# A planner with a stricter PSUM rule and another transfer model, and 48 sums made by GpSimd instead of VectorE

## The chip, the cores and the metric

The kernel runs on one core of a Trainium2 chip. A core has five engines that run side by side, each in the order of its own queue: TensorE (matrix products, "PE" in the profile, with its weight loads as "PEld"), VectorE ("DVE"), ScalarE ("ACT"), GpSimd ("POOL") and SyncE ("SP"), which here only issues transfers. Operands lie in SBUF, 128 partitions wide; TensorE writes its sums into PSUM. What is measured is the device time of one execution, in microseconds (us). Comparisons use the median of several executions.

## The reference

The kernel computes a gated mix of two branches over the same `x` (2048 rows, 1024 columns), all in fp32:

```python
g = sigmoid((x * gate_w).sum(-1, keepdims=True))
a = x @ hid_re.T;  b = x @ hid_im.T              # [2048, 1024] each
A = seq_re @ a - seq_im @ b                      # real part of the 2-D Fourier mixing
h = relu(x @ w1 + b1) ** 2                       # [2048, 3584]
B = h @ w2 + b2
out = g * A + (1 - g) * B
```

The four matrices of the Fourier part come in as inputs. The result is needed in fp32 accuracy.

## The kernel before, in words

**Products.** TensorE multiplies in a reduced fp32 format, so every fp32 operand is split in two: `hi`, a copy rounded to that format (ScalarE, `Operand.sum_parts`, line 297), and `lo = operand - hi` (VectorE, `Operand.rest_parts`, line 306). A product of two operands is three matrix products, hi·lo, hi·hi and lo·hi. To do fewer of them the kernel uses Strassen's scheme in Winograd's form: seven products of half-sized blocks instead of eight, with four sums on the left side (`SUMS_L`: S1 to S4), four on the right (`SUMS_R`: T1 to T4, lines 36 to 39), and adds of the results. Many of the seven products are themselves made by the same scheme once more ("twice", second level); the others are made directly.

**Stages.** The work is four matrix products one after the other: x (x times the hidden Fourier matrices, function `x_stage`), c (the sequence Fourier matrices times that, `c_stage`), h in two parts (x times `w1`, `h_stage`), and o (`w2` times h, `o_stage`). Stages x and h run through `wide`, c and o through `tall`. In each the seven products are done in the order 1, 2, 5, 6, 3, 7, 4. In `tall` the constants `TWICE_C` and `TWICE_O` (line 21) say which are done twice and over how many of their k-steps: in c products 1 (one double step), 2, 3 and 4 (four double steps each, which is all of them); in o product 1 (two) and 2, 3 and 4 (three double steps, six of the seven k-steps). What is left of the k-steps (`rest` in `tall.twice`, lines 523 to 532) is done plainly: before the second level when the product starts from nothing or is named in `FIRST_C` / `FIRST_O` (line 22), otherwise after it. With `rest` done first, an extra set of PSUM groups takes it up and writes it to SBUF, and the second level is put on top. With `rest` done last, its matrix products go into the same PSUM groups as the second level's products 2, 3 and 4, and into a fourth group for the block (1, 1) (lines 614 to 636). The last product of the last stage (o, product 4) ends in a group that hands over each of its two rows by itself (`by_row`, lines 608 to 610); which group that is depends on whether `rest` comes last.

**One second level step.** For each double step q of a twice-product in `tall`, the left operand's blocks lie in two tiles, and `l2[q]` (line 543) makes the sums S1 to S4 of their halves, each 128x512 elements (two tiles of 256 columns). S1 and S3 take two loaded blocks, S2 needs S1, S4 needs S2. The sum itself is issued in `Part.make_parts` (line 257), by VectorE. In stages c and o that is 13 + 11 = 24 double steps. The right sums are 128x1024 each.

**PSUM.** PSUM is used as four pools, each a tile of 128x2x512 fp32, so of two rows of 128x512. A group's result is taken up by VectorE or ScalarE. In o's `final` (line 881) the two rows of a tile are finished by two `scalar_tensor_tensor` instructions (bias and gate), one per row, then one add of the whole tile, and the tile goes out through a store on GpSimd's queue. `last` (line 866) does the same for a single row, with the store on SyncE's or ScalarE's queue.

**The order of the work.** Nothing is issued while the program is described: every instruction is recorded as an `Op` (line 99) with its time by a table of costs (lines 27 to 30), and with the earlier ops that it must follow (`Queue`, lines 139 to 146). `plan` (line 973) then gives every op a due time, counted back from the matmuls, which are to run without a pause, and simulates the engines: when an engine is free it takes the ready op that is due first. Matmuls keep their recorded order. SBUF is 55 slots of 128x1024 fp32; a tile gets its slot in the order of due time less a lead (`LEAD`), and a load can't be issued before its tile has a slot. `emit` writes the instructions out in the order of the planned starts, one fixed queue per engine. The engines then run for real in these orders, with waits wherever a tile is shared, so what the plan gets wrong shows up as a wait. All instructions carry the line of the call in `emit`, L1125, so the profile tells them apart by tile names: `raw` is a loaded block, `sum` a sum, `hi`, `lo` the halves of an operand (`both` for the 256-wide ones), `ps` a PSUM tile, `u`, `ab`, `y`, `h`, `o` results, `copy` a sum kept in DRAM.

Of the kernel before, what the change touches and what calls it, by code (L numbers as in the profile page):

```python
# [15 lines left out]
P = 128  # L16
# [2 lines left out]
SLOTS = 55  # L19
WIDE, TALL_C, TALL_O = ((1, 2, 5, 6, 3, 7, 4),) * 3  # L20
TWICE_X, TWICE_C, TWICE_O = (1, 2, 5, 3, 4), {1: 1, 2: 4, 3: 4, 4: 4}, {1: 2, 2: 3, 3: 3, 4: 3}
FIRST_C, FIRST_O = (2,), (2, 4)
WARM = 44
FAR_TALL, FAR_WIDE = ("T2",), ()
TWICE_H = (1, 2, 5, 3, 4), (1, 2, 5, 3, 4)

MM, MM_END, FIRST_MM = 0.2267, 0.18, 6.2
VEC, VEC_END, ACT, ACT_END = (0.086, 1.0417e-3), 0.39, (0.11, 0.89e-3), 0.36
ISSUE, RING, RATE, SEM, LANES = {"sync": 0.36, "scalar": 0.36, "gpsimd": 0.56}, (1.1, 1.1), 400e3, 0.06, 8
LEAD = {"raw": 5.0, "hi": 5.0, "sum": 5.0, "out": 0.0}  # L30

ADD, SUB = ALU.add, ALU.subtract

# [2 lines left out]
SUMS_L = {"S1": ((1, 0), (1, 1), ADD), "S2": ("S1", (0, 0), SUB), "S3": ((0, 0), (1, 0), SUB),  # L36
          "S4": ((0, 1), "S2", SUB)}
# [7 lines left out]
def gated_mix_kernel(ctx: ExitStack, tc: tile.TileContext, x4, xn, w4, ct, w1a, w1b, w2, b1, b2, gw, out):  # L45
# [11 lines left out]
    class Sight:  # L57


        def __init__(self, base, chain, box):  # L60
            self.base, self.chain, self.box = base, chain, box
# [12 lines left out]
        def __getattr__(self, name):  # L74
            def later(*args, **kwargs):
                return Sight(self.base, self.chain + (lambda t: getattr(t, name)(*args, **kwargs),), self.box)
            return later
# [21 lines left out]
    class Op:  # L99


        def __init__(self, engine, name, args, kwargs):
            self.engine, self.name, self.args, self.kwargs = engine, name, args, kwargs
            sights = [a for a in (*args, *kwargs.values()) if isinstance(a, Sight)]
            outs = [a for a in (args[0], kwargs.get("accum_out")) if isinstance(a, Sight)]
            self.ins, self.outs = [a for a in sights if not any(a is o for o in outs)], outs
            n = max([a.size() for a in sights] + [0])
            self.load, self.end = 0.0, 0.0
            if name == "dma_start":
                self.time, self.load = ISSUE[engine], n * P * 4 / RATE  # L110
            elif engine == "tensor":
                self.time, self.end = (MM, MM_END) if n >= 512 else (0.13, 0.1)
            elif engine == "scalar":
                self.time, self.end = ACT[0] + ACT[1] * n + (1.3 if args[2] == AF.Sigmoid else 0.0), ACT_END
            elif name == "tensor_scalar":
                self.time, self.end = VEC[0] + VEC[1] * n / 2, VEC_END
            else:
                self.time, self.end = VEC[0] + VEC[1] * n, VEC_END
            self.after, self.then, self.new, self.latest, self.landed = set(), [], [], None, False
# [3 lines left out]
    class Queue:  # L123
# [5 lines left out]
        def __getattr__(self, name):  # L129
            def record(*args, **kwargs):  # L130
                op = Op(self.engine, name, args, kwargs)
                op.latest = urgent[0]
                for sight, write in [(a, False) for a in op.ins] + [(a, True) for a in op.outs]:
                    block = sight.base
                    if not block.seen and block.home in ("slot", "bank"):
                        op.new.append(block)
                    if not block.seen and block.before is not None:
                        op.after.update(o for o, *_ in block.before.seen)
                    for other, box, wrote in block.seen:
                        if (write or wrote or block.home == "bank") and (not box or not sight.box or (  # L140
                                box[0] < sight.box[1] and sight.box[0] < box[1] and (
                                    block.home == "bank" or box[2] < sight.box[3] and sight.box[2] < box[3]))):
                            op.after.add(other)
                    block.seen.append((op, sight.box, write))
                op.after.discard(op)
                ops.append(op)
                return op
            return record
# [4 lines left out]
    nc = Machine()  # L153
# [19 lines left out]
    def take(name, dtype=F32):  # L173
        return Block(name, dtype, "slot")
# [50 lines left out]
    class Part(Near):  # L225


        def __init__(self, a, b=None, op=None, width=512):
            super().__init__("part")
            self.blocks, self.op, self.width, self.copy = ([a] if b is None else [a, b]), op, width, None  # L230
            self.cuts = [(slice(0, 2), slice(0, width))]
            for e in self.blocks:
                if isinstance(e, (Near, View)):
                    e.uses += 1
# [14 lines left out]
        def make_parts(self):  # L249
            for b in self.blocks:  # L250
                assert not isinstance(b, (Near, View)) or b.done
            src = [b.slot if isinstance(b, (Near, View)) else t for b, t in zip(self.blocks, self.slots)]
            mine = [t for t in self.slots if t is not None]
            self.slot, self.done = mine[0] if mine else take("sum"), True
            for k, c in self.cuts:
                if self.op:
                    nc.vector.tensor_tensor(self.slot[:, k, c], src[0][:, k, c], src[1][:, k, c], op=self.op)
                yield
            for b in self.blocks:
                if isinstance(b, (Near, View)):  # L260
                    b.used()
            if self.copy:
                stores.append((self.copy, self, 0, 2))
# [53 lines left out]
    class Half:  # L317
# [6 lines left out]
        hi = property(lambda self: self.base.hi[:, :, self.at:self.at + 256])  # L324
# [70 lines left out]
    class Sums:  # L395


        def __init__(self, get, sums, keep=False, far=()):

            self.get, self.sums, self.keep, self.far, self.made = get, sums, keep, far, {}  # L400

        def of(self, key, width=512, near=False):
            if key in self.made:
                return self.made[key]
            if key not in self.sums:
                if not self.keep:
                    return self.get(*key)
                b = self.get(*key)
                e = b if isinstance(b, (Near, View)) else Part(b, width=width)
            else:  # L410
                a, b, op = self.sums[key]
                e = Part(*(self.of(p, width).far() if p in self.far and not near else self.of(p, width) for p in (a, b)), op, width)
            self.made[key] = e
            return e

# [55 lines left out]
    def tall(left, right, ksteps, order, second, first, target, final, last=None):  # L471
# [46 lines left out]
        def twice(p, old, new, ends, drop, sign):  # L518
# [3 lines left out]
            k = second[p]  # L522
# [16 lines left out]
            def near(b):  # L539
                return b if isinstance(b, Near) else Part(b)  # L540

            base = {(j, q): near(left[2 * q + j].of(l)) for j in range(2) for q in range(k)}
            l2 = {q: Sums(lambda m, j, q=q: View(base[j, q], 256 * m), SUMS_L, True) for q in range(k)}
            r2 = {q: Sums(lambda j, c, q=q: right[2 * q + j, c].of(r), SUMS_R, True) for q in range(k)}

            def one(_, ps):
# [88 lines left out]
            for e in own:  # L635
                step(*e)

        return seven(order, second, lambda: {k: Near("u") for k in keys}, c11, c12, c21, c22, put, add, direct, twice, 2)

    def wide(left, right, rows, order, second, target, final, sign=1, onto_old=False):  # L640
# [264 lines left out]
    at, rows = c_stage()  # L905
# [5 lines left out]
    at, rows, fetched, ends = o_stage()  # L911
# [31 lines left out]
    ideal, t = [], FIRST_MM  # L943
# [29 lines left out]
def plan(ops, count, start):  # L973

    t = start
# [20 lines left out]
    def lead(op, block):  # L996
        kind = "raw" if op.load else "out" if any(a.base.home == "bank" for a in op.ins) else "hi"
        return op.due - LEAD[kind]

# [10 lines left out]
    moving, at, version = {}, 0.0, 0  # L1010
    lanes = [], []

    def push(t, *what):
        heappush(events, (t, len(events) + 1e-9 * len(order), id(what), what))
# [5 lines left out]
    def loosen(op):  # L1020
        op.wait -= 1
        if not op.wait:
            able(op)

    def hand_out():
        nonlocal head
        while head < len(queue) and free:
# [2 lines left out]
            head += 1  # L1030
            loosen(op)

    def flow(t):
        nonlocal at, version
        for e in moving:
            moving[e][1] -= (t - at) / len(moving)
        at = t
        version += 1
        for e in [e for e in moving if moving[e][1] <= 1e-9]:
            op = moving.pop(e)[0]  # L1040
            push(t + RING[1], "done", op)
        for e, r in rings.items():
            if e not in moving and r:
                op = r.popleft()
                moving[e] = [op, op.load]
        if moving:
            push(t + max(0.0, min(m[1] for m in moving.values())) * len(moving), "flow", version)

    def finish(op):
        op.landed = True  # L1050
# [116 lines left out]
```

## Time and profile before

| | us |
|---|---|
| median of 3 executions (1870.84 to 1874.90) | 1872.18 |
| the profiled execution | 1871.76 |
| its span, first to last instruction | 1869.6 |
| TensorE busy | 1852.4 |
| VectorE busy | 1761.1 |
| ScalarE busy | 1086.2 |
| GpSimd busy | 87.6 |

The profile is of one execution. Its rows give the time that each engine worked, and the idle time ahead of an instruction with what ended it ("<-DVE o" means that VectorE's last write or read of a tile `o` released it). A matmul record lasts about 390 ns while the next starts after about 227 ns, since matmuls are pipelined; so a pause of TensorE is read from the distance between starts. In the timeline each line has the start, the length, the engine, the operation, the tiles and, in brackets, the idle time just before. In a table by stretches each engine has its busy time and, in brackets, its instructions.

The boundaries of the products in stage o, by counting matmuls (one product of 300, three of 336, and so on) back from the last: product 1 about 1356 to 1427, product 2 to 1495, product 5 to 1571, product 6 to 1648, product 3 to 1719, product 7 to 1795, product 4 to the end. In stage c, which ends about 863, product 3 takes about 623 to 700.

### The profile page before, as it was taken

To read this page: it belongs to the slowest core of one execution; us is meant where nothing else is said; L and a number is where in the kernel's file an instruction comes from. 1 tells how busy PE (TensorE), PEld (TensorE's weight loads), DVE (VectorE), ACT (ScalarE), POOL (GpSimd) and SP (SyncE) were. 2 spreads that over 40 slices of the span, in tenths; PEclk is the share of its full clock that TensorE was granted. 3 is DMA by queue.
4 is the path that set the end of the run, shared out by engine and by line. 5 is a ranking of instruction groups with operands and counts; after the bars stand their busy time and mean duration, and the time that the engine had idled before them with its cause. 6 is when DMAs were issued, how large, how long until landed. Compare 5 with 4: busy or idle time off the path is not lost. (4 is left out here: it accounts for less than half of the span.)

```text
span 1869.6 us, 22164 instructions
## 1 busy us (share of the span) xinstructions
PE 1852.4 (99%) x8162; PEld 1529.5 (82%) x8162; DVE 1761.1 (94%) x1728; ACT 1086.2 (58%) x1231; POOL 87.6 (5%) x162
## 2 busy tenths in 40 slices
PE   9999999999999999999999999999999999999998
PEld 7888888888888888888888888788887888887887
DVE  8997998999889899999997999999999998989988
ACT  6474554563343554466584798767977435364462
POOL 0000100000000000000000001000010000000000
PEclk9999999999999999999999999999999999999999
DMA  4641979449798379444551845737664798649952
GB/s 180 259 169 67 352 264 385 159 152 409 266 324 324 136 268 411 158 166 168 219 198 56 333 170 184 270 122 284 240 240 172 288 386 317 269 146 380 363 180 90
DMA packets 128860, 445.04 MB, mean 238 GB/s; under 512 B 14176, under 2 KB 23664, under 8 KB 128752
## 3 DMA queue, kind: packets, MB, share of 16 engines
q1 hardware_dynamic: 106848, 365.10, 53.1%
q0 software_dynamic: 21616, 78.14, 10.6%
q8 instruction: 64, 1.05, 0.2%
q10 hardware_dynamic: 288, 0.39, 0.1%
q14 instruction: 44, 0.36, 0.1%
HBM read 364.92 MB, written 78.65 MB: 237 GB/s over the span
## 5 line engine op out<-in xcount | busy, mean ns | idle before, releaser
L1125 PE MATMUL ps<-hi 128*128 128x512 f32 x2034 | 793.5, 391 | 6.5 <-DVE h L1125 2.6
L1125 PE MATMUL ps<-hi,lo 128*128 128x512 f32 x2034 | 792.9, 390 | 1.7 <-DVE o L1125 1.7
L1125 PE MATMUL ps<-lo,hi 128*128 128x512 f32 x2034 | 792.4, 390 | 0.0
L1125 ACT ACTIVATE hi<-raw 128x1024 fp32r<-128x1024 f32 (+2 forms) x384 | 394.2, 1037 | 341.7 <-DVE raw L1125 212.1
L1125 DVE TENSOR_TENSOR lo<-raw,hi 128x1024 fp32r<-128x1024 f32 (+2 forms) x384 | 454.1, 1200 | 13.4 <-ACT hi L1125 10.7
L1125 PEld LDWEIGHTS ps<-hi 128*128 128x128 f32 x2034 | 382.5, 188 | 88.9 <-ACT hi L1125 4.0
L1125 PEld LDWEIGHTS ps<-hi,lo 128*128 128x128 f32 x2034 | 382.5, 188 | 82.7 <-DVE o L1125 2.6
L1125 PEld LDWEIGHTS ps<-lo,hi 128*128 128x128 f32 x2034 | 382.5, 188 | 79.5 <-DVE lo L1125 0.2
L1125 PE MATMUL ps<-hi,both 128*128 128x512 f32 x1344 | 416.1, 390 | 2.5 <-ACT ps L1125 2.5
L1125 DVE TENSOR_TENSOR raw<-raw 128x1024 f32<-128x1024 f32 (+1 forms) x276 | 327.6, 1209 | 28.1 <-DMA raw<-in_ct 11.7
L1125 ACT ACTIVATE hi<-sum 128x1024 fp32r<-128x1024 f32 x216 | 219.6, 1034 | 157.5 <-DVE sum L1125 111.0
L1125 PEld LDWEIGHTS ps<-hi,both 128*128 128x128 f32 x1344 | 252.3, 188 | 56.1 <-ACT ps L1125 3.8
L1125 DVE TENSOR_TENSOR lo<-sum,hi 128x1024 fp32r<-128x1024 f32 (+1 forms) x216 | 255.1, 1198 | 13.5 <-PE ps L1125 7.4
L1125 PE MATMUL ps<-lo,both 128*128 128x512 f32 x672 | 261.7, 389 | 0.0
L1125 DVE TENSOR_TENSOR sum<-raw 128x1024 f32<-128x1024 f32 (+2 forms) x156 | 160.9, 1041 | 8.3 <-PE ps L1125 4.4
L1125 ACT ACTIVATE u<-ps 128x1024 f32<-128x1024 f32 (+1 forms) x116 | 112.2, 972 | 71.4 <-PE ps L1125 53.6
L1125 PEld LDWEIGHTS ps<-lo,both 128*128 128x128 f32 x672 | 126.2, 188 | 26.0
L1125 DVE TENSOR_TENSOR sum<-raw,sum 128x1024 f32<-128x1024 f32 (+2 forms) x117 | 128.7, 1103 | 7.2 <-PE ps L1125 6.1
L1125 DVE TENSOR_TENSOR h<-h,ps 128x1024 f32<-128x1024 f32 (+1 forms) x92 | 98.7, 1085 | 8.7 <-ACT u L1125 6.2
L1125 ACT ACTIVATE ps<-u 128x1024 f32<-128x1024 f32 (+1 forms) x84 | 82.1, 980 | 29.2 <-DVE o L1125 7.4
L1125 ACT ACTIVATE both<-sum 128x512 fp32r<-128x512 f32 x96 | 59.3, 626 | 66.0 <-DVE sum L1125 54.0
L1125 ACT ACTIVATE h<-h,b1c 128x512 f32<-128x512 f32 x112 | 75.7, 710 | 10.0 <-DVE h L1125 9.9
(47 smaller groups left out, 731.5 us busy)
## 6 DMA issues: line engine op xcount, KB each, us to landing
raw<-in_ct SPq DMA_DIRECT2D x153, 512.0 KB, 6.7
raw<-h SPq DMA_DIRECT2D x134, 512.0 KB, 7.3
raw<-in_x SPq DMA_DIRECT2D x107, 512.0 KB, 5.5
raw<-in_w SPq DMA_DIRECT2D x98, 512.0 KB, 7.1
raw<-ab SPq DMA_DIRECT2D x72, 512.0 KB, 7.1
h<-h POOLq DMA_DIRECT2D x48, 512.0 KB, 5.3
raw<-in_w1a SPq DMA_DIRECT2D x36, 512.0 KB, 6.2
ab<-ab POOLq DMA_DIRECT2D x32, 512.0 KB, 7.0
```

The source lines that it names most:

```text
L1125: made = getattr(real[op.engine], op.name)(*(actual(a) for a in op.args), **{k: actual(v) for k, v in op.kwargs.items()})
```

## The change

Five edits in one:

1. `FIRST_O` loses product 4: its left-over k-step is now done after the second level, as product 3's is. So the kernel's last group becomes the block (1, 1) with one k-step (12 matmuls), after three groups of 12 matmuls that end blocks (0, 0), (1, 0) and (0, 1).
2. In the recording of dependencies, any two accesses to the same PSUM tile are now ordered in the plan, reads against reads and the two rows of a tile against each other. Before, only accesses to overlapping rows were.
3. ScalarE is counted as 0.11 + 0.84e-3 n (before 0.89e-3) with 0.41 at the end (0.36). A transfer is counted with 1.6 us ahead and 2.0 behind (1.1 and 1.1), at 405e3 bytes per us alone and 370e3 shared (400e3).
4. Tiles that are loaded get their slot 9 us ahead of the due time, not 5.
5. S1 and S3 of the second level in `tall` are issued on GpSimd: 24 double steps, two sums each, 48 adds of 128x512. The plan counts each as 0.3 + 2.2e-3 n.

```diff
-FIRST_C, FIRST_O = (2,), (2, 4)
+FIRST_C, FIRST_O = (2,), (2,)
...
-VEC, VEC_END, ACT, ACT_END = (0.086, 1.0417e-3), 0.39, (0.11, 0.89e-3), 0.36
-ISSUE, RING, RATE, SEM, LANES = {"sync": 0.36, "scalar": 0.36, "gpsimd": 0.56}, (1.1, 1.1), 400e3, 0.06, 8
-LEAD = {"raw": 5.0, "hi": 5.0, "sum": 5.0, "out": 0.0}
+VEC, VEC_END, ACT, ACT_END = (0.086, 1.0417e-3), 0.39, (0.11, 0.84e-3), 0.41
+ISSUE, RING, RATE, SEM, LANES = {"sync": 0.36, "scalar": 0.36, "gpsimd": 0.56}, (1.6, 2.0), (405e3, 370e3), 0.06, 8
+POOL = 0.3, 2.2e-3
+LEAD = {"raw": 9.0, "hi": 5.0, "sum": 5.0, "out": 0.0}
...
-                self.time, self.load = ISSUE[engine], n * P * 4 / RATE
+                self.time, self.load = ISSUE[engine], n * P * 4 / RATE[0]
...
+            elif engine == "gpsimd":
+                self.time, self.end = POOL[0] + POOL[1] * n, VEC_END
...
-                        if (write or wrote or block.home == "bank") and (not box or not sight.box or (
-                                box[0] < sight.box[1] and sight.box[0] < box[1] and (
-                                    block.home == "bank" or box[2] < sight.box[3] and sight.box[2] < box[3]))):
+                        if block.home == "bank" or (write or wrote) and (not box or not sight.box or (
+                                box[0] < sight.box[1] and sight.box[0] < box[1] and box[2] < sight.box[3]
+                                and sight.box[2] < box[3])):
                             op.after.add(other)
...
-        def __init__(self, a, b=None, op=None, width=512):
+        def __init__(self, a, b=None, op=None, width=512, adder=nc.vector):
             super().__init__("part")
+            self.adder = adder
...
-                    nc.vector.tensor_tensor(self.slot[:, k, c], src[0][:, k, c], src[1][:, k, c], op=self.op)
+                    self.adder.tensor_tensor(self.slot[:, k, c], src[0][:, k, c], src[1][:, k, c], op=self.op)
...
-        def __init__(self, get, sums, keep=False, far=()):
+        def __init__(self, get, sums, keep=False, far=(), other=()):
+            self.other = other
...
-                e = Part(*(self.of(p, width).far() if p in self.far and not near else self.of(p, width) for p in (a, b)), op, width)
+                e = Part(*(self.of(p, width).far() if p in self.far and not near else self.of(p, width) for p in (a, b)), op, width,
+                         nc.gpsimd if key in self.other else nc.vector)
...
-            l2 = {q: Sums(lambda m, j, q=q: View(base[j, q], 256 * m), SUMS_L, True) for q in range(k)}
+            l2 = {q: Sums(lambda m, j, q=q: View(base[j, q], 256 * m), SUMS_L, True, other=("S1", "S3")) for q in range(k)}
...
+    def share():
+        return 1.0 if len(moving) == 1 else len(moving) * RATE[0] / RATE[1]
+
     def flow(t):
         nonlocal at, version
         for e in moving:
-            moving[e][1] -= (t - at) / len(moving)
+            moving[e][1] -= (t - at) / share()
...
-            push(t + max(0.0, min(m[1] for m in moving.values())) * len(moving), "flow", version)
+            push(t + max(0.0, min(m[1] for m in moving.values())) * share(), "flow", version)
```

## The prediction

> **What bounds the kernel now.** I read the page first, then the table by stretches, the waits of TensorE, and the timeline around each of its pauses.
>
> ```profile
> span 1869.6 us, 22164 instructions
> PE 1852.4 (99%) x8162; PEld 1529.5 (82%) x8162; DVE 1761.1 (94%) x1728; ACT 1086.2 (58%) x1231; POOL 87.6 (5%) x162
> ```
> ```profile
> core 0: us, PE busy (x) PEld busy (x) DVE busy (x) ACT busy (x) POOL busy (x), PEclk, DMA share, GB/s
> 288.80:863.40 574.60, 574.60 (x2536) 475.93 (x2536) 537.82 (x543) 282.82 (x317) 17.07 (x32) 1.00 0.68 255
> 1427.00:1495.20 68.20, 68.20 (x302) 56.52 (x301) 67.77 (x76) 41.14 (x50) 0.71 (x1) 1.00 0.66 241
> 1647.60:1719.00 71.40, 68.86 (x301) 56.04 (x300) 68.27 (x72) 38.51 (x44) 0.09 (x1) 1.00 0.67 248
> 1141.00:1353.00 212.00, 208.22 (x914) 170.96 (x913) 203.20 (x211) 165.21 (x210) 14.01 (x26) 1.00 0.62 222
> 630.00:716.00 86.00, 86.00 (x381) 71.25 (x380) 85.69 (x90) 48.16 (x56) 1.60 (x3) 1.00 0.68 260
> ```
>
> TensorE works 1852.4 of 1869.6 us, always at the full granted clock, and the number of its matmuls does not change. So no edit can win more than its pauses. In stage c (288.8 to 863.4) there is none at all. Stage o's product 2 (1427 to 1495) shows the unhindered pace: 300 matmuls in 68.20 us, 0.227 us each. Product 3 has 300 too and takes 71.40 us: 3.2 us of pauses. VectorE is the second bound. It works 67.77 of 68.20 us in o's product 2, 85.69 of 86.00 around c's product 3: where both levels of sums are made it has no time of its own left, and the kernel lives on the lead it built up before.
>
> How small that lead becomes is read by pairing an operand's `lo` with the matmul that takes it, in the queues' fixed orders. These are the tightest pairs, first in c's product 3, then in o's product 2:
>
> ```profile
> 671.94 1.29 DVE L1125 TENSOR_TENSOR both<-raw,both 128x512 fp32r<-128x512 f32 x2
> 676.00 0.61 PE L1125 MATMUL ps<-hi,both 128*128 128x512 f32 x2
> ...
> 1489.80 0.69 DVE L1125 TENSOR_TENSOR both<-sum,both 128x512 fp32r<-128x512 f32 x1
> 1492.95 0.62 PE L1125 MATMUL ps<-hi,both 128*128 128x512 f32 x2
> ```
>
> The first of the two at 671.94 ends at 672.6, its matmul starts at 676.0: 3.4 us. In o it is 2.5 us. VectorE may fall back that far, less some 0.3 us of handover, before TensorE stops.
>
> **The change, part by part.**
>
> *The PSUM rule.* Product 3 of o has these pauses:
>
> ```profile
> 1706.93 0.39 PE L1125 MATMUL ps<-lo,hi 128*128 128x512 f32 x1
> 1707.35 0.75 DVE L1125 SCALAR_TENSOR_TENSOR o<-ps,b2c,g 128x512 f32<-128x512 f32 x1 [0.23 <-PE ps L1125]
> ...
> 1708.16 0.50 PE L1125 MATMUL ps<-hi,lo 128*128 128x512 f32 x1 [0.85 <-DVE o L1125]
> ...
> 1711.57 0.51 PE L1125 MATMUL ps<-hi 128*128 128x512 f32 x1 [0.84 <-DVE o L1125]
> ...
> 1715.25 0.51 PE L1125 MATMUL ps<-hi,lo 128*128 128x512 f32 x1 [0.84 <-DVE o L1125]
> ```
>
> Six matmuls fill row 0 of a tile, VectorE starts to read row 0, and TensorE then waits with row 1 of the same tile until that read has ended. The old plan let VectorE in between because the rows differ; the built program makes TensorE wait for the whole tile. Under the new rule the first `scalar_tensor_tensor` follows row 1's matmuls, so all three pauses go: minus 3.2 us by the table. What is late next is the block's end, by row 1's six matmuls (1.36 us); product 7 behind it needs a tile only after the next group's 2.7 us, which covers that.
>
> *Product 4 of o, left-over step last.* It loses a set of groups: four copies into PSUM, four out, against one copy more at the end, all on ScalarE, which works 36.5 us in the last 74 and covers either. Its second-level products then follow in the order 2, 4, 3 (block (1, 0) before (0, 1)) where now 4 comes last. That hits one pause:
>
> ```profile
> 1841.08 1.03 ACT L1125 ACTIVATE ps<-o 128x1024 f32<-128x1024 f32 x1 [2.28 <-DVE o L1125]
> 1841.20 0.39 PE L1125 MATMUL ps<-hi,both 128*128 128x512 f32 x1
> 1842.16 0.50 PE L1125 MATMUL ps<-hi,both 128*128 128x512 f32 x1 [0.57 <-ACT ps L1125]
> ```
>
> Here block (0, 1)'s copy is needed 2.7 us after product 5 has ended; later it is needed after 5.4. The pause is 1842.16 − 1841.20 − 0.23 = 0.7 us, and goes. Cost: the end.
>
> ```profile
> 1857.62 1.40 DVE L1125 SCALAR_TENSOR_TENSOR o<-ps,b2c,g 128x512 f32<-128x512 f32 x2
> ...
> 1859.06 1.22 DVE L1125 TENSOR_TENSOR o<-o,raw 128x1024 f32<-128x1024 f32 x1
> ...
> 1863.83 0.39 PE L1125 MATMUL ps<-hi,both 128*128 128x512 f32 x1
> 1864.29 0.74 DVE L1125 SCALAR_TENSOR_TENSOR o<-ps,b2c,g 128x512 f32<-128x512 f32 x1
> 1865.07 0.69 DVE L1125 TENSOR_TENSOR o<-o,raw 128x512 f32<-128x512 f32 x1
> 1865.79 0.35 ACTq L1125 DMA_DIRECT2D out<-o  x1
> ```
>
> Call T the end of the last matmul's turn, 1863.83 + 0.23 = 1864.06. Now the last row is done at 1865.76 = T + 1.7, and the span ends 3.8 us after that. In the new order three blocks end 8.2, 5.4 and 2.7 us before T, each 1.40 + 1.22 = 2.6 us of VectorE. The third starts 0.2 us after its matmuls and ends at T + 0.2. Only then come the two rows, 1.45 us each: T + 3.1. The end is 1.4 us later. The third block's store on GpSimd's queue starts well before the last row's and is covered by it. The left-over step's sums and `lo` move from the start of product 4 to its end, so nothing is due earlier; its loads move likewise.
>
> *48 sums to GpSimd.*
>
> ```profile
> L1125 DVE TENSOR_TENSOR sum<-raw 128x512 f32<-128x512 f32 x48 | 33.0, 688 | 1.7 <-PE ps L1125 1.1 <-DMA raw<-ab 0.5
> L1125 POOL DMA_DIRECT2D copy<-raw x30 | 16.0, 534 | 179.9 <-DVE raw L1125 179.9
> ```
>
> VectorE is relieved of 33.0 us: 8 sums or 5.5 us in each four-step product of c, 6 or 4.1 us in o's products 2, 3 and 4, 4 or 2.75 us in o's product 1. In c that buys nothing now, as TensorE never waits there. It does in o's product 1:
>
> ```profile
> 1407.48 0.63 ACT L1125 ACTIVATE both<-raw 128x512 fp32r<-128x512 f32 x1 [1.87 <-DMA raw<-in_w]
> 1408.09 0.39 PE L1125 MATMUL ps<-hi,both 128*128 128x512 f32 x1
> 1409.08 0.50 PE L1125 MATMUL ps<-hi,both 128*128 128x512 f32 x1 [0.60 <-ACT ps L1125]
> ...
> 1411.71 0.39 PE L1125 MATMUL ps<-hi,both 128*128 128x512 f32 x1
> 1412.21 2.34 DVE L1125 TENSOR_TENSOR u<-u,ps 128x1024 f32<-128x1024 f32 x2
> 1413.47 0.50 PE L1125 MATMUL ps<-hi,both 128*128 128x512 f32 x1 [1.37 <-ACT ps L1125]
> ```
>
> The pause at 1413.47 is 1.5 us; ScalarE's copy waits for VectorE's backlog of adds. 2.75 us less ahead of them takes it away. What GpSimd needs for such a sum no row shows; its only rows are descriptor work for stores, 0.53 us each. Bounds: VectorE's own 0.69, and, as an outer end, 2.4, twice VectorE's 1.22 for a tile of double size; quicker than 0.69 would change nothing, since GpSimd is idle there (one 0.53 us store in o's product 2, three in 630 to 716). I take the 1.43 that the plan books. As a stretch of GpSimd's own time this is covered: 8 x 1.43 = 11 us in a product of 76. GpSimd's queue also holds the stores, and a sum behind a store waits until VectorE has made that tile, but the plan places both by the same clock and, as the table shows, few stores fall there. What is open is whether VectorE and GpSimd can both read SBUF at full speed; no row shows it, since GpSimd reads no operand now. It is the main rival below.
>
> The Trainium skill speaks against this edit: its page "SBUF — State Buffer", section "Who interferes with whom", says that a VectorE instruction with two SBUF inputs and a GpSimd instruction that reads SBUF shut each other out for a whole instruction. No row of this trace can confirm it. The page "GPSIMD Engine Reference", section "Performance versus the Vector engine", gives 4497 ns for an add of 2048 elements, so by estimate 1.1 us for 512; with the lock at that length the rival's sum would come to about 1871.3.
>
> *Transfers, lead, ScalarE's cost.* The plan gave a load 3.5 us; the page has more:
>
> ```profile
> raw<-in_ct SPq DMA_DIRECT2D x153, 512.0 KB, 6.7
> q1 hardware_dynamic: 106848, 365.10, 53.1%
> ```
>
> With 4.9 to 5 us and 4 us more lead, loads are issued some 5.4 us earlier. 365.1 MB are 696 tiles; 696 x 5.4 / 1870 = 2 of the 55 slots more taken by loads on average, so a little less lead for sums, covered while leads are over 2.5 us. It should spare the pause at 1409.08 (0.8 us), where ScalarE's queue stood 1.87 us at a late load of `w2` with the needed copy behind it. The bounds of the whole re-planning are in stage h's second part:
>
> ```profile
> 1195.66 1.22 DVE L1125 TENSOR_TENSOR h<-h,ps 128x1024 f32<-128x1024 f32 x1
> 1197.03 0.47 PE L1125 MATMUL ps<-hi 128*128 128x512 f32 x1 [1.76 <-DVE h L1125]
> 1288.18 0.47 PE L1125 MATMUL ps<-hi 128*128 128x512 f32 x1
> ```
>
> Five times a PSUM tile is read by VectorE and at once used again; it costs 2.0 us where another VectorE instruction had just begun (1197.03), and 0.3 at best (1288.18). All together now cost 5.0; a new order can make it 1.5 to 10. I count zero and keep minus 3.5 and plus 5 for the range.
>
> *Sum,* from the profiled execution's 1871.76: − 3.2 − 0.7 − 1.5 − 0.8 + 1.4 = 1867.0. The median stands 0.4 above that execution: 1867.4.
>
> **The rivals.**
>
> *VectorE is held up by GpSimd's sums* (the other side). For: VectorE has no idle time where the sums stand, and it loses more than it gains if a sum shuts it out for longer than 0.69. Against: no row shows such a hold. At 1.43 each sum costs 0.74 net. c's product 3: 8 x 0.74 − 3.1 = 2.8 us of new pauses; o's product 2: 6 x 0.74 − 2.2 = 2.2; o's product 1, already late: 4 x 0.74 = 3.0, and its 1.5 us pause stays. 1867.4 + 9.5 = 1876.9. It decides from about 1.2 us per sum, where 18 x 0.5 − 5.3 + 1.5 eats the 4.8 us of gain.
>
> *Only the PSUM repair counts.* The pauses in o's product 1 stay or come back elsewhere: 1872.2 − 3.2 − 0.7 + 1.4 = 1869.7. For: ScalarE's late load and VectorE's backlog there depend on the order, which is drawn anew.
>
> *The rule does not do what it says:* the reads still slip between the rows, and product 4, now built like product 3, gets the same 3.2: 1867.4 + 6.4 = 1873.8. Against: with row 1's matmuls among its predecessors the read can't be planned ahead of them.
>
> **How the numbers follow.** Forecast 0.42, held-up VectorE 0.30, repair only 0.20, rule without effect 0.08. The range runs from 1862, the forecast with stage h at its best and some early pauses gone, to 1880, the hold at 1.6 us. 0.2%, or 3.7 us, is about what a measurement of this kernel can tell from no change: faster 0.43 (the forecast and the lower edge of the repair), slower 0.32 (the hold and some of the last), same 0.25. The forecast's own range is 1863 to 1870.
>
> **What would show it.** TensorE: no pause inside a tile at o's product 3, none at its product 4; the two rows' ends about 3 us behind the last matmul. GpSimd: 48 adds; if they or VectorE's 1.22 us instructions grow longer where both work, the hold is real, and pauses on `lo` or `both` in c's product 3 would follow. The prediction is wrong if new pauses appear where the lead was thin, or if stage h's second part changes by more than 3 us.

## The result, and the profile after

| | before | changed |
|---|---|---|
| median, us | 1872.54 | 1887.69 |
| the profiled execution, us | 1871.76 | 1885.56 |
| its span, us | 1869.6 | 1883.8 |

The changed kernel takes 1.008 times as long (95% interval 1.0067 to 1.0093): 15 us slower where 5 us faster was forecast, and outside the range. The page after, its span, its engines and one group that was not there before:

```profile
span 1883.8 us, 22249 instructions
PE 1856.8 (99%) x8162; PEld 1529.5 (81%) x8162; DVE 1765.6 (94%) x1680; ACT 1076.2 (57%) x1224; POOL 189.3 (10%) x210
L1134 POOL TENSOR_TENSOR sum<-raw 128x512 f32<-128x512 f32 x48 | 101.0, 2108 | 346.0 <-PE ps L1134 139.5
```

VectorE has 48 instructions fewer, which took 33.0 us before, and yet works 4.5 us longer. A sum on GpSimd takes 2.1 us on average, not the 1.43 that the plan books. By stages (x, c, h, o, with the boundaries where the matmul counts put them), first before, then after; the first number behind a stretch is its length, the second TensorE's busy time:

```profile
289.30:863.20 573.90, 573.90 (x2533) 475.36 (x2532) 537.12 (x543) 282.82 (x317) 17.02 (x32) 1.00 0.68 255
863.20:1353.90 490.70, 486.92 (x2143) 401.81 (x2142) 469.46 (x445) 372.30 (x444) 31.14 (x59) 1.00 0.57 208
1353.90:1869.60 515.70, 505.23 (x2221) 416.24 (x2219) 486.51 (x497) 267.33 (x304) 23.11 (x38) 1.00 0.69 257
```
```profile
289.00:870.40 581.40, 575.42 (x2533) 474.88 (x2532) 536.27 (x517) 280.33 (x316) 72.86 (x58) 1.00 0.67 253
870.40:1362.10 491.70, 487.86 (x2143) 401.43 (x2142) 468.71 (x444) 375.12 (x450) 32.84 (x62) 1.00 0.58 206
1362.10:1883.80 521.70, 508.70 (x2221) 418.25 (x2219) 492.16 (x475) 256.67 (x291) 66.81 (x57) 0.99 0.66 251
```

Stage c is 7.5 us longer, stage o 6.0, h 1.0. These are the two stages that hold the sums. What TensorE waited for, after:

```profile
PE ps L1134 <- ACT ps L1134: 12.1, 10, 2.8
PE ps L1134 <- DVE h L1134: 3.1, 5, 1.2
PE ps L1134 <- DVE lo L1134: 1.3, 2, 1.1
```

Ten waits, 12.1 us, for ScalarE's copies into PSUM; waits for `lo`, where the prediction had looked for trouble, are 1.3, both in stage x and so ahead of the first sum on GpSimd. The copies themselves are held up by VectorE. At the end of the second level in c's product 4, before (product starts at 787.1) and after (791.2), VectorE and ScalarE:

```profile
825.07 1.22 DVE L1125 TENSOR_TENSOR y<-u,ps 128x1024 f32<-128x1024 f32 x1
...
828.78 1.22 DVE L1125 TENSOR_TENSOR u<-u,ps 128x1024 f32<-128x1024 f32 x1
830.04 1.23 DVE L1125 TENSOR_TENSOR y<-u 128x1024 f32<-128x1024 f32 x1
...
831.52 1.01 ACT L1125 ACTIVATE ps<-y 128x1024 f32<-128x1024 f32 x1
```
```profile
833.02 1.21 DVE L1134 TENSOR_TENSOR y<-u,ps 128x1024 f32<-128x1024 f32 x1
...
836.73 1.22 DVE L1134 TENSOR_TENSOR u<-u,ps 128x1024 f32<-128x1024 f32 x1
837.99 1.22 DVE L1134 TENSOR_TENSOR y<-u 128x1024 f32<-128x1024 f32 x1
...
839.24 1.03 ACT L1134 ACTIVATE ps<-y 128x1024 f32<-128x1024 f32 x1 [2.02 <-DVE y L1134]
...
840.32 0.50 PE L1134 MATMUL ps<-hi,both 128*128 128x512 f32 x1 [1.96 <-ACT ps L1134]
```

It is the same run of instructions in the same order, but the second `u<-u,ps` starts 41.7 us into the product before and 45.5 after. So VectorE is not doing other work there; it does the same work 3.8 us later. Why it is late shows where a GpSimd sum meets it:

```profile
641.93 0.68 DVE L1134 TENSOR_TENSOR both<-sum,both 128x512 fp32r<-128x512 f32 x1
642.08 1.68 POOL L1134 TENSOR_TENSOR sum<-raw 128x512 f32<-128x512 f32 x1 [2.90 <-DVE lo L1134]
642.53 2.31 DVE L1134 TENSOR_TENSOR lo<-sum,hi 128x1024 fp32r<-128x1024 f32 x1
```

GpSimd's sum is ready at 642.08 but lasts 0.4 us longer than its shortest kin (1.28), as VectorE is just reading; VectorE's `lo`, begun at 642.53, lasts 2.31 instead of 1.22. Over the whole trace the 56 instructions of 128x1024 with both inputs in SBUF that overlap a sum last 1.67 us on average, up to 2.54; the other 998 last 1.22, and so do the 8 that overlap one but have an input in PSUM (1.21).

### The profile page after: what moved, and what is told of

Same layout as the page of the kernel before. It is cut to its first block, busy times and chain, and to the rows that moved or that the text cites. A ratio compares the mean times of both kernels' runs of the same rounds, so it can differ in the third digit from the quotient of the medians.

```text
span 1883.8 us, 22249 instructions
## 1 busy us (share of the span) xinstructions
PE 1856.8 (99%) x8162; PEld 1529.5 (81%) x8162; DVE 1765.6 (94%) x1680; ACT 1076.2 (57%) x1224; POOL 189.3 (10%) x210
## 5 line engine op out<-in xcount | busy, mean ns | idle before, releaser
L1134 PE MATMUL ps<-hi,both 128*128 128x512 f32 x1344 | 420.6, 392 | 12.4 <-ACT ps L1134 12.1
L1134 DVE TENSOR_TENSOR raw<-raw 128x1024 f32<-128x1024 f32 (+1 forms) x276 | 324.4, 1203 | 12.1 <-DMA raw<-in_ct 4.9
L1134 DVE TENSOR_TENSOR lo<-sum,hi 128x1024 fp32r<-128x1024 f32 (+1 forms) x216 | 264.0, 1237 | 19.4 <-PE ps L1134 9.2
L1134 DVE TENSOR_TENSOR sum<-raw,sum 128x1024 f32<-128x1024 f32 (+2 forms) x117 | 133.6, 1144 | 3.6 <-PE ps L1134 2.6
L1134 POOL TENSOR_TENSOR sum<-raw 128x512 f32<-128x512 f32 x48 | 101.0, 2108 | 346.0 <-PE ps L1134 139.5
L1134 DVE TENSOR_TENSOR sum<-raw 128x1024 f32<-128x1024 f32 x108 | 130.8, 1223 | 4.0 <-DMA raw<-in_x 2.1
L1134 ACT ACTIVATE ps<-u 128x1024 f32<-128x1024 f32 (+1 forms) x80 | 78.0, 977 | 23.9 <-DVE u L1134 7.1
```

The costliest lines, as they stand in the source:

```text
L1134: made = getattr(real[op.engine], op.name)(*(actual(a) for a in op.args), **{k: actual(v) for k, v in op.kwargs.items()})
```

## The experiments

Two theories. *Hold:* a GpSimd sum and a VectorE instruction with two SBUF inputs shut each other out, VectorE falls behind a plan that does not know it, and its adds out of PSUM, which have no lead, come late. *Re-planning:* the new transfer, lead and ScalarE numbers put these adds too late in the order. Medians below stand beside the kernel before in the same comparison, 1872.2 to 1872.3.

**The changed kernel with the sums back on VectorE.**

```diff
-            l2 = {... SUMS_L, True, other=("S1", "S3")) for q in range(k)}
+            l2 = {... SUMS_L, True) for q in range(k)}
```

> The changed kernel with S1 and S3 back on VectorE, all else as changed. Theory 'hold' (a GpSimd sum and a VectorE instruction with two SBUF inputs shut each other out, so VectorE falls behind its plan and its adds out of PSUM come late): the pauses at the ends of the twice-products in stages c and o go, 1866 to 1873 us. Rival 're-planning' (the new transfer, lead and ScalarE numbers put the adds too late in the order): the pauses stay, 1883 to 1889 us.

1867.24 us, ratio 0.9973 (0.9962 to 0.9984). Its stage c, and its o products 1 and 3:

```profile
290.40:864.30 573.90, 573.90 (x2534) 475.20 (x2533) 535.08 (x541) 280.55 (x316) 16.20 (x31) 1.00 0.67 253
1354.90:1425.60 70.70, 70.70 (x313) 58.56 (x312) 70.32 (x77) 49.94 (x62) 3.23 (x6) 1.00 0.62 230
1645.90:1713.90 68.00, 68.00 (x301) 56.31 (x301) 67.61 (x72) 39.33 (x45) 0.00 (x0) 1.00 0.69 257
```

No pause in any. The sums on GpSimd alone are worth 20.4 us of loss; everything else in the change gains 5.

**The kernel before with the sums on GpSimd, nothing else** (the `adder` and `other` lines of the change and its `POOL` cost).

> The kernel before with S1 and S3 on GpSimd and counted at 1.43 us, nothing else. 'Hold': pauses of 2 to 4 us in c's products 2 to 4 and o's products 1, 2 and 4 as in the changed kernel, 1880 to 1892 us; 128x1024 adds of VectorE that fall on a GpSimd sum last 1.5 to 2.5 us against 1.22. 'Re-planning': 1869 to 1875 us.

1897.54 us, ratio 1.0132 (1.0117 to 1.0147): 25 us slower, above the expected range. Its copies into PSUM keep TensorE waiting as in the changed kernel; the second line has the three row reads of o's product 3, which were there before, and three more around the end of product 2:

```profile
PE ps L1130 <- ACT ps L1130: 14.1, 10, 3.0
PE ps L1130 <- DVE o L1130: 6.1, 6, 1.8
```

**The PSUM rule alone.**

```diff
-                        if (write or wrote or block.home == "bank") and (not box or not sight.box or (
+                        if block.home == "bank" or (write or wrote) and (not box or not sight.box or (
...
```

> The kernel before with the PSUM rule alone. Both theories: the three pauses of o's product 3 (3.2 us) go and little else changes, 1868 to 1871 us. If the order of everything shifts with it, up to 3 us either way in stage h's second part.

1869.07 us, ratio 0.9981 (0.9971 to 0.9990). Its o product 3 takes 68.00 us against 71.40; in the profiled execution, the quickest of the ten (1866.27), product 1 gains 1.6 as well (71.7 against 73.3), by the new order:

```profile
1353.40:1425.10 71.70, 71.11 (x314) 58.53 (x314) 69.65 (x75) 51.76 (x67) 4.86 (x9) 1.00 0.62 226
1645.40:1713.40 68.00, 68.00 (x302) 56.31 (x301) 67.86 (x73) 37.53 (x44) 0.72 (x1) 1.00 0.64 240
```

**The left-over step last, alone.**

```diff
-FIRST_C, FIRST_O = (2,), (2, 4)
+FIRST_C, FIRST_O = (2,), (2,)
```

> The kernel before with the left-over step of o's product 4 done last, alone. The end is 1.4 us later, the 0.7 us pause at 1842 goes, and without the PSUM rule the row-by-row reads pause product 4's last groups as they pause product 3's, up to 3.2 us: 1873 to 1877 us.

1874.52 us, ratio 1.0013 (1.0004 to 1.0022). Without the PSUM rule the row-by-row reads now stop TensorE in product 4 as well, six waits where there were three:

```profile
PE ps L1125 <- DVE o L1125: 5.1, 6, 0.8
```

**The transfer, lead and ScalarE numbers alone** (the lines `ACT`, `RING`, `RATE`, `LEAD` and `share`).

> The kernel before with the transfer, lead and ScalarE numbers of the changed one alone. 'Hold': within 4 us of before, 1868 to 1876, since these numbers only reorder. 'Re-planning' would have asked for 1880 and more.

1869.13 us, ratio 0.9984 (0.9974 to 0.9993). Re-planning falls: these numbers gain, and where the forecast had put it, in o's product 1 (73.3 us before, from 1353.9 to 1427.2):

```profile
1353.80:1424.50 70.70, 70.70 (x313) 58.56 (x312) 69.97 (x76) 49.88 (x62) 3.24 (x6) 1.00 0.63 233
```

**The hold without the relief: an extra add on GpSimd beside each of VectorE's 48.** It reads the same two blocks and writes a spare tile (in bf16, for room).

```diff
+                    if self.adder is nc.gpsimd:
+                        nc.gpsimd.tensor_tensor(spare, src[0][:, k, c], src[1][:, k, c], op=self.op)
```

> The kernel before, all its sums on VectorE, and beside each of the 48 S1 and S3 a GpSimd add of the same two blocks into a spare tile that nobody reads. The hold without the relief. If reading is what holds: VectorE's two-input instructions on SBUF last up to 2.5 us where they meet one, those with an input in PSUM stay at 1.22, and the time is above the kernel with the sums merely moved (1897.5): 1900 to 1925 us. If it is not the reading: below 1880.

**The same with a write alone.**

```diff
+                    if self.adder is nc.gpsimd:
+                        nc.gpsimd.memset(spare, 0.0).after.add(made)
```

> The same with a GpSimd memset of the spare tile in place of the add: GpSimd writes SBUF and reads nothing. If reading is what holds: VectorE's instructions keep 1.22 us and the time is 1869 to 1876 us. If any GpSimd work in SBUF holds: above 1885.

1900.28 us (ratio 1.0149, 1.0134 to 1.0165) and 1871.64 (0.9997, 0.9987 to 1.0007). The engines' line of the page and TensorE's wait for copies, with the reading adds, then with the writes:

```profile
PE 1861.5 (98%) x8162; PEld 1531.9 (81%) x8162; DVE 1805.4 (95%) x1728; ACT 1085.6 (57%) x1231; POOL 200.4 (11%) x210
PE ps L1133 <- ACT ps L1133: 18.6, 12, 3.8
```
```profile
PE 1851.0 (99%) x8162; PEld 1527.6 (82%) x8162; DVE 1760.9 (94%) x1728; ACT 1087.2 (58%) x1231; POOL 113.2 (6%) x210
PE ps L1133 <- ACT ps L1133: 3.0, 4, 1.6
```

VectorE has the same 1728 instructions in both and works 44.5 us longer beside the reads: 0.93 us for each of the 48. It is the reading that holds. The writes cost nothing that can be measured; they are shorter (0.53 us each) and lie elsewhere in time, but the 28 two-input instructions of 128x1024 that overlap one kept their 1.22 us. The reading kernel is only 2.7 us slower than the one with the sums moved, so the 33 us of relief were worth almost nothing. Nobody reads the spare tile, so no engine waits for a late GpSimd sum here: such waits are not needed for the loss.

**The changed kernel, with a plan that books the hold.**

```diff
+            if e == "gpsimd" and not op.load:
+                late = max(0.0, idle["vector"] - t)
+                op.time += late
+                idle["vector"] = t + late + HOLD      # HOLD = 1.1
+                push(idle["vector"], "wake")
```

> The changed kernel, GpSimd's sums kept, but the plan books the hold: a sum starts when VectorE is free and keeps VectorE for 1.1 us. If the loss is that VectorE's adds come later than the plan puts them, most of the pauses go though VectorE has no less to do: 1868 to 1878 us. If the loss is VectorE's time itself, the pauses stay: 1882 to 1890.

1870.10 us, ratio 0.9990 (0.9981 to 1.0000). The engines' line of its page, and its stage c:

```profile
PE 1850.3 (99%) x8162; PEld 1526.7 (82%) x8162; DVE 1768.9 (95%) x1680; ACT 1076.3 (58%) x1224; POOL 189.1 (10%) x210
289.10:863.00 573.90, 573.90 (x2533) 475.17 (x2532) 536.46 (x513) 279.48 (x315) 72.24 (x57) 1.00 0.67 253
```

VectorE works 3.3 us longer than in the changed kernel, and the kernel is 17.6 us faster. So the loss was not VectorE's working time but the place of its instructions: with the hold known, the plan does the adds in time and lets the operands' `lo`, which have a lead, wait. One thing more changed with the plan. In the changed kernel VectorE also stood still for sums that GpSimd had not finished, five times, 8.4 us in all. Four of the five:

```profile
DVE sum L1134 <- POOL sum L1134: 7.2, 4, 2.4
```

With the hold booked these waits are 2.4 us. How much of the 17.6 us comes from them is not shown. The sums on GpSimd still cost 2.9 us against leaving them on VectorE (1867.24).

**A longer sum in the plan, but no hold.**

```diff
-POOL = 0.3, 2.2e-3
+POOL = 0.3, 3.5e-3
```

> The changed kernel with a GpSimd sum booked at 0.3 + 3.5e-3 n, 2.1 us for 512, which is its measured mean, but no hold of VectorE in the plan. If the plan only had the sums too short: 1868 to 1874 us. If it is VectorE's standing still that the plan lacks: pauses as in the changed kernel, 1882 to 1892.

1884.49 us, ratio 1.0067 (1.0053 to 1.0081). Copies into PSUM still cost 11.5 us. The sum's own length is not what the plan lacked:

```profile
PE ps L1134 <- ACT ps L1134: 11.5, 8, 2.0
```

**Half the sums, S1 alone.**

```diff
-            l2 = {... SUMS_L, True, other=("S1", "S3")) for q in range(k)}
+            l2 = {... SUMS_L, True, other=("S1",)) for q in range(k)}
```

> The changed kernel with S1 alone on GpSimd, 24 sums instead of 48. 'Hold' in proportion: about half of the 20.4 us between the changed kernel (1887.7) and the one with no sum on GpSimd (1867.2): 1874 to 1881 us. If the lead still covers half the dose: 1867 to 1871.

1870.73 us, ratio 0.9988 (0.9979 to 0.9997): 3.5 us above no sum on GpSimd, not half of 20.4. The loss is not in proportion to the sums: 24 of them are mostly absorbed, 48 are not. Whether the number decides, or that S1 and S3 of a step lie close together, is not shown.

**All but the sums and the left-over step.** The changed kernel with its sums on VectorE and `FIRST_O` as before.

> The changed kernel with its sums on VectorE and product 4 of o left-over step first, as before: the PSUM rule and the transfer, lead and ScalarE numbers alone. The forecast's step on the end (1.4 us for three blocks crowding the end, 0.7 us back from a pause) says 0.7 us under the kernel with that step last, 1867.2: 1865 to 1868. If the order of the end costs nothing: 1867 to 1869.

1866.06 us, ratio 0.9968 (0.9955 to 0.9980): the fastest kernel here, 6.3 us under the kernel before in the same comparison and 1.2 under the one with the left-over step last.

## Why the prediction was wrong

*The PSUM rule:* right. o's product 3 was to lose 3.2 us; it takes 68.40 us after against 71.40, with no pause inside a tile:

```profile
1660.10:1728.50 68.40, 68.29 (x301) 56.23 (x301) 68.33 (x69) 38.00 (x43) 5.26 (x4) 1.00 0.71 263
```

*Product 4, the end:* the mechanism was right and the size close. The last row was to be done at T + 3.1. After:

```profile
1875.93 1.22 DVE L1134 TENSOR_TENSOR o<-o,raw 128x1024 f32<-128x1024 f32 x1
1877.08 0.74 DVE L1134 SCALAR_TENSOR_TENSOR o<-ps,b2c,g 128x512 f32<-128x512 f32 x1
...
1878.46 0.74 DVE L1134 SCALAR_TENSOR_TENSOR o<-ps,b2c,g 128x512 f32<-128x512 f32 x1
1879.24 0.69 DVE L1134 TENSOR_TENSOR o<-o,raw 128x512 f32<-128x512 f32 x1
```

The last matmul starts at 1876.78, so T is 1877.0 and the row is done at 1879.9, T + 2.9: 1.2 us instead of 1.4. The pause of 0.7 us that was to go is replaced by one of 2.1 us, again at the second of the copies into PSUM. In the new order that is the copy of block (1, 0), and it waits for late adds; with the sums on VectorE there is no such pause. Net the forecast had this edit at 0.7 us of loss; the two kernels without GpSimd sums that differ in it alone stand 1.2 apart (1867.24 and 1866.06).

*48 sums to GpSimd:* the step that failed. The prediction counted them as covered on GpSimd and as 2.75 us less ahead of o's product 1's adds, a gain of 1.5 us, and put the hold at nothing. The runs show a loss of 20.4 us in their place (1887.69 with them, 1867.24 without). VectorE is relieved of 0.69 us per sum and stretched by 0.80 (1765.6 less the 1760.1 − 33.0 that it would have worked, over 48). The Trainium skill's rule was right here (page "SBUF — State Buffer", section "Who interferes with whom": a VectorE instruction with two SBUF inputs and a GpSimd reader shut each other out). The trace agrees with 2.31 against 1.22 us, and in the run with writes alone nothing was stretched. The rival had the right mechanism with a chance of 0.30, and gave 1876.9. It was too cheap because it looked at the wrong lead. The 3.4 and 2.5 us between a `lo` and its matmul held, but the chain of adds at the end of a second level, `u<-u,ps`, `y<-u`, then a copy into PSUM, has almost none, and there VectorE's whole lateness falls on TensorE, in c's products 2, 3 and 4 and in o's 1, 2 and 4. So it priced three products where six lose. The three that it left out, c's products 2 and 4 and o's product 4, take this in the changed kernel:

```profile
373.30:451.80 78.50, 76.76 (x337) 62.90 (x336) 78.17 (x79) 40.68 (x50) 5.66 (x4) 1.00 0.66 243
791.20:870.40 79.20, 76.73 (x337) 62.88 (x336) 77.78 (x80) 45.38 (x54) 11.46 (x8) 1.00 0.47 169
1804.70:1877.00 72.30, 70.21 (x301) 57.11 (x299) 69.10 (x72) 32.36 (x39) 7.08 (x8) 0.98 0.36 129
```

With the sums on VectorE they take 76.2, 76.2 and 68.6 us, counted in the same way: 9.0 us to which the rival gave nothing. The three that it priced, c's product 3 and o's 1 and 2, lose 9.1 us against its 9.5. That these agree is partly luck, since its price for a sum was not what happened: it took VectorE's net loss as 0.74 us, and measured it is 0.11. It may be that the plan had counted on the relief, so that against it VectorE falls behind by 0.69 and 0.80 together, up to 1.5 us per sum by this estimate. That is not shown: beside the reading adds, where the plan counted on no relief, VectorE is stretched by 0.93 us per sum, and the kernel loses no less (28.1 us against 25.2 with the sums moved).

*Transfers, lead, ScalarE:* right in sign, and larger than counted: alone, they clear both pauses of o's product 1 (0.8 and 1.5 us), of which the second had been put down to the relief. Stage h's second part stayed within the range given: 5.2 us of pauses before, 4.5 after.

Without the failed step the sum stands: the forecast was 1867.4, and the change less its GpSimd sums is 1867.24. That the two agree so closely is partly luck, since the relief's 1.5 us came from another edit.

## What to carry to other kernels

Moving work to an idle engine can slow the busy one: look first whether the two hold each other up, as GpSimd's reads of SBUF and VectorE's instructions with two inputs in SBUF do here. A plan that does not know of such a hold was hurt more here by the lateness than by the lost time, so either book it (17.6 us back here) or leave the work where it is. And when you ask how late an engine may run, ask it of every instruction that hands something over, not only of those with the most visible lead: the add that must free or refill an accumulator had almost none here.

## What the runs showed of the hardware

After two of these pauses TensorE ran slow. Between the first 20 us and the last matmul of this trace the granted clock changes at 1423.23, 1426.65, 1843.07 and 1846.48, all whole multiples of 3.413 us apart. The stretches below are cut on the same grid, two for each of the four longest pauses; TensorE's busy time is the second number, the granted clock the third from the end:

```profile
1419.82:1423.23 3.41, 0.63 (x3) 0.41 (x3) 3.38 (x4) 1.50 (x2) 0.00 (x0) 1.00 0.18 71
1423.23:1426.65 3.42, 3.42 (x10) 2.64 (x9) 3.35 (x4) 1.41 (x3) 0.00 (x0) 0.50 0.00 0
1839.65:1843.07 3.42, 1.48 (x7) 0.92 (x6) 3.39 (x4) 1.79 (x3) 0.00 (x0) 1.00 0.28 114
1843.07:1846.48 3.41, 3.41 (x10) 2.63 (x9) 3.41 (x4) 2.54 (x3) 0.00 (x0) 0.50 0.00 0
836.14:839.56 3.42, 2.23 (x10) 1.50 (x8) 3.28 (x4) 1.40 (x3) 0.00 (x0) 1.00 0.98 383
839.56:842.97 3.41, 2.65 (x11) 2.17 (x12) 3.41 (x4) 3.26 (x5) 0.00 (x0) 1.00 0.01 4
672.31:675.72 3.41, 1.66 (x7) 1.39 (x8) 3.41 (x4) 2.63 (x3) 0.00 (x0) 1.00 0.77 268
675.72:679.13 3.41, 3.41 (x16) 2.83 (x16) 3.41 (x5) 1.99 (x3) 0.00 (x0) 1.00 0.40 131
```

The pauses that end at 1422.77 (2.78 us of idle) and 1842.63 (1.94) lie whole in one stretch, and in the next the clock stands at 0.50 and seven matmuls come 0.43 us apart instead of 0.23, 1.4 us more. The pause of 1.96 us that ends at 840.32 is as long as the second of them, but the grid splits it into 1.19 and 0.76, and the clock stays at 1.00; so it does after 674.06, with 1.75 us of idle in its stretch. The thirteen traces of this case agree over the same part: the clock fell to half 13 times, each time behind a stretch with 1.84 us of idle or more, and of the stretches that it did not fall behind only one had more than 1.76 (1.87, in the run with the reading adds). So a pause of about 2 us can cost another 1.4, if it falls into one stretch of the grid. The Trainium skill, page "TensorE: Matmul & The Clock Gate", section "Why this matters for your kernels", warns of gaps over some 3 us; here less was enough.

The hold works both ways: GpSimd's sum takes 1.28 us at its quickest and 6.28 at its slowest (from 1448.23), with VectorE's instructions back to back:

```profile
L1134 POOL TENSOR_TENSOR sum<-raw x48: 1278/1644/6284, 313.0 to 1811.0; 128x512 f32<-128x512 f32 x48
```
